# Two PSUM banks per VectorE instruction in the last stage of a recurrence-and-mixture kernel

## The chip, the cores and the metric

The kernel runs on one core of one Trainium2 chip. The metric is the device time of one execution in microseconds, as the median of several runs; lower is better. Beside it there is one profiled execution, whose trace gives the time of every instruction and every DMA packet.

The engines are named as in the profile: PE is TensorE's matrix multiplication (PEld its weight load), DVE is VectorE, ACT is ScalarE, POOL is GpSimd and SP is SyncE, which here only issues DMAs. "SPq L834" is the queue of SP at line 834.

## The reference

Two layers in sequence. The first is a gated recurrence over time; the second is a mixture of experts in which every token is softly assigned to 32 slots (8 experts of 4 slots).

```python
# x, f_logit: (4, 5056, 256); lower_bound: (256,)
sig = 1.0 / (1.0 + np.exp(-f_logit))
f = lower_bound + (1.0 - lower_bound) * sig
for t in range(S):
    h = f[:, t] * h + (1.0 - f[:, t]) * x[:, t]
    y[:, t] = h
# y as (20224, 256); phi: (256, 32); w1: (8, 256, 1024); w2: (8, 1024, 256)
logits = y @ phi
d = softmax of logits over the tokens        # each slot's mix of tokens
slot_out = for each expert e: relu((d.T @ y)[e] @ w1[e]) @ w2[e]
c = softmax of logits over the 32 slots      # each token's mix of slots
out = c @ slot_out                           # (20224, 256), float32
```

The change concerns the last line alone: the 20,224 output rows of 256 floats, 20.71 MB, are products of the tokens' weights (32 numbers a token) with the 32 slot outputs, divided by the sum of the token's weights.

## The kernel before

**Up to the last stage.** `x` and `f_logit` are read in pieces, the recurrence runs as scans on VectorE, and TensorE turns tokens and channels and collects the slots' inputs. The experts follow, in the pools `pm`, `pbig` and others. What the last stage needs then lies in SBUF: `etall`, the exponentials of all logits (128 partitions: 4 batches of 32 slots; one column a position in the sequence); `rrow`, the reciprocals of the row sums; `slot_out`, the slot outputs, repeated for each batch; and `slot_bd`, the same in a two-block layout in which a pair of batches shares 64 partitions, so that one matmul gives the rows of two batches (L759, made by GpSimd).

**How the output is tiled.** `blocks` cuts the sequence of 5056 positions into two blocks of 2048 (`n_r` = 16 rows on each of 128 partitions), one of 896 (`n_r` = 7) and 64 left-over positions. A partition holds `n_r` neighbouring positions, so a store writes `n_r` KB in one piece for each partition.

**What one step does.** TensorE multiplies into one bank of PSUM (128 x 512 floats, 2 KB a partition). Then VectorE or ScalarE reads the bank, multiplies by the reciprocals of the row sums and writes to an SBUF tile. `by_vector` (L765, 766) does a whole bank with one instruction, with the scale as a second operand that is repeated along the row. `by_scalar` (L768 to 770) does one instruction for each row of 256, with the scale as a number for each partition. `next_engine` alternates between the two, bank by bank. When the tile is full, SP issues its store.

**The order**, written out at L853 to 862, is also the order on every engine (the schedule is manual):

1. `pieces(0, 3)`: the first block of batch 3, whose first three rows are stored earlier, in five small stores (10 banks).
2. `couple(2, 0)` and `couple(2, 1)`: the block of 7 rows for batches 0 and 1, then 2 and 3 (7 banks each, two stores of 0.9 MB each).
3. `rest()`: the 64 left-over positions of all batches (2 banks). ScalarE copies half of each bank (L847), VectorE adds the other half (L848), and one VectorE instruction scales them (L849). Two small stores.
4. `whole(0, 2)`: the first block of batch 2 (16 rows, 8 banks of two rows, one store of 2.10 MB).
5. `couple(0, 0)`, `couple(1, 0)`, `couple(1, 1)`: the remaining long blocks in pairs of batches (16 banks of one row of two batches each; two stores of 2.10 MB each).

**Buffers.** `pout` holds 8 tiles of one bank, all of PSUM, handed out in turn by `bank()`. With `reuse_waits="tile"`, a tile of a new pool waits for the earlier users of its own banks and not for everything in the pools that lay there. SBUF holds three tiles for single batches (`ob`) and three for pairs (`oc`), from the pool `osb`.

Of the kernel before, what the change touches and what calls it, by code (L numbers as in the profile page):

```python
# [9 lines left out]
F32 = mybir.dt.float32  # L10
# [4 lines left out]
PSUM = bass.MemoryType.PSUM  # L15
# [3 lines left out]
def kernel(  # L19
# [10 lines left out]
    nc = tc.nc  # L30
    B, S, D = x.shape
    E = moe_w1.shape[0]
    F = moe_w1.shape[2]
    NS = moe_phi.shape[1]
    SPE = NS // E
    P = 128
# [25 lines left out]
    blocks = [(i * P * wide_r, wide_r) for i in range(n_blk)]  # L62
# [57 lines left out]
    etall = store.tile([P, S + PAD], BF16, name="etall")[:, :S]  # L120
    rrow = store.tile([P, n_grp * R, B], F32, name="rrow")
# [6 lines left out]
    slot_bd = store.tile([P, 2, D], BF16, name="slot_bd")  # L128
# [39 lines left out]
    with tc.tile_pool(name="sp2", bufs=3) as sp2, \  # L168
# [430 lines left out]
        for o in range(DC):  # L599
            nc.tensor.matmul(sin_ps[:, o], slot_v[:, o], rep[:, 0],  # L600
                             start=True, stop=True, skip_group_check=True)
# [3 lines left out]
    with tc.tile_pool(name="ew", bufs=1) as ew, \  # L605
# [18 lines left out]
        for q in range(E // Q):  # L624
            hi = ew.tile([P, F], BF16, name=f"hi{q}")
            for k in range(2):
                hi_ps = (psu.tile([P, H], F32, name="hi_ps", tag="up") if q == 0 else
                         pbig.tile([P, H], F32, name="hi_ps", tag=f"hi_ps{k}"))
                for o in range(DC):
                    for j in range(Q):  # L630
                        nc.tensor.matmul(hi_ps[ds(j * NS, NS)], sin[:, o],
                                         w1_sb[q * Q + j][:, o, ds(k * H, H)],
                                         start=(o == 0), stop=(o == DC - 1),
                                         skip_group_check=True)
# [7 lines left out]
        for q in range(E // Q):  # L642
# [6 lines left out]
            k = Q if q == 0 else Q - 1  # L649
# [38 lines left out]
        for i in range(n_late):  # L688
# [3 lines left out]
                             start=True, stop=True, skip_group_check=True)  # L692
# [20 lines left out]
        q = n_grp * R - 1  # L713
        for i in range(len(blocks)):
            expert(Q + i)
            row_sums(i)
            if i < len(blocks) - 1:
                spin(so_ps, 3, D)
                k = ds(i * wide_r, wide_r)
# [3 lines left out]
        k = len(blocks) - 1  # L723
# [39 lines left out]
    with tc.tile_pool(name="osb", bufs=3, reuse_waits="tile") as osb:  # L763

        def by_vector(ob, op, scale):  # L765
            nc.vector.tensor_tensor(ob, op, scale.broadcast_to(list(ob.shape)), ALU.mult)  # L766

        def by_scalar(ob, op, scale):  # L768
            for i in range(ob.shape[1]):
                nc.scalar.activation(ob[:, i], op[:, i], ACT.Copy, scale=scale[:, i])  # L770

        def share(op, i, b, r, k):
            t0, n_r = blocks[i]
            ew = etall[ds(b * NS, NS), ds(t0, P * n_r)].rearrange("s (p r) -> s p r", r=n_r)
            for j in range(k):
                nc.tensor.matmul(op[:, j], ew[:, :, r + j], slot_out[ds(b * NS, NS)],
                                 start=True, stop=True, skip_group_check=True)

        def scale_of(i, b, r, k):
            return rrow[:, ds(blocks[i][0] // P + r, k), ds(b, 1)]  # L780

        def rows_of(i, b):
            t0, n_r = blocks[i]
            return out[ds(b * S + t0, P * n_r)].rearrange("(p r) d -> p r d", r=n_r)

        pout = ctx.enter_context(
            tc.tile_pool(name="pout", bufs=8, space=PSUM, reuse_waits="tile"))

        def bank():
            return pout.tile([P, 2, D], F32, name="op", tag="op")  # L790

        def pieces(i, b):
            dst = rows_of(i, b)
            ob = osb.tile([P, blocks[i][1], D], F32, name="ob", tag="ob")
            for r, ks in ((3, (1, 1)), (5, (1, 1)), (7, (1, 1)), (9, (2, 2)), (13, (2, 1))):
                q = r
                for k, by in zip(ks, (by_vector, by_scalar)):
                    op = bank()
                    share(op, i, b, q, k)
                    by(ob[:, ds(q, k)], op[:, ds(0, k)], scale_of(i, b, q, k))  # L800
                    q += k
                nc.sync.dma_start(out=dst[:, ds(r, q - r)], in_=ob[:, ds(r, q - r)])

        turn = [0]

        def next_engine():
            turn[0] += 1
            return turn[0] % 2

        def whole(i, b):  # L810
            n_r = blocks[i][1]
            ob = osb.tile([P, n_r, D], F32, name="ob", tag="ob")
            for r in range(0, n_r, 2):
                k = min(2, n_r - r)
                op = bank()
                share(op, i, b, r, k)
                (by_scalar, by_vector)[next_engine()](
                    ob[:, ds(r, k)], op[:, ds(0, k)], scale_of(i, b, r, k))
            nc.sync.dma_start(out=rows_of(i, b), in_=ob)

        def couple(i, j):
            t0, n_r = blocks[i]
            ew = etall[ds(j * 2 * NS, 2 * NS), ds(t0, P * n_r)].rearrange(
                "s (p r) -> s p r", r=n_r)
            ob = osb.tile([P, 2, n_r, D], F32, name="oc", tag="oc")
            for r in range(n_r):
                op = bank()
                nc.tensor.matmul(op.rearrange("p u d -> p (u d)"), ew[:, :, r],  # L828
                                 slot_bd[ds(j * 2 * NS, 2 * NS)].rearrange("s u d -> s (u d)"),
                                 start=True, stop=True, skip_group_check=True)  # L830
                (by_scalar, by_vector)[next_engine()](
                    ob[:, :, r], op, rrow[:, t0 // P + r, ds(2 * j, 2)].unsqueeze(2))
            for u in range(2):
                nc.sync.dma_start(out=rows_of(i, 2 * j + u), in_=ob[:, u])  # L834

        def rest():
            n_p = B // 2
            ob = osb.tile([P, n_p, D], F32, name="ob", tag="ob")
            dst = out.rearrange("(b t) d -> t b d", b=B)
            for j in range(n_p):  # L840
                k = ds(j * 2 * NS, 2 * NS)
                op = bank()
                nc.tensor.matmul(op.rearrange("p u d -> p (u d)"),
                                 left[k].rearrange("s t u -> s (t u)"),
                                 slot_bd[k].rearrange("s u d -> s (u d)"),
                                 start=True, stop=True, skip_group_check=True)
                nc.scalar.copy(ob[:, j], op[:, 0])  # L847
                nc.vector.tensor_tensor(ob[:, j], ob[:, j], op[:, 1], ALU.add)  # L848
            by_vector(ob, ob, rrow[:, n_grp * R - 1, ds(0, n_p)].unsqueeze(2))  # L849
            for j in range(n_p):  # L850
                nc.sync.dma_start(out=dst[ds(S - L, L), ds(2 * j, 2)], in_=ob[:, j])

        pieces(0, B - 1)  # L853
        end = len(blocks) - 1
        couple(end, 0)
        couple(end, 1)
        rest()
        whole(0, B - 2)
        for i in range(end):
            for j in range(B // 2):  # L860
                if i or j < B // 2 - 1:
                    couple(i, j)


# [28 lines left out]
```

## Time and profile before

| | |
|---|---|
| median of 3 runs | 197.41 us (197.39 to 197.84) |
| the profiled execution, time | 197.27 us |
| its span, first to last instruction | 195.5 us |
| bytes written | 20.71 MB |
| first packet of the output | 144.04 us from the span's start |
| last packet of the output | 193.1 us |
| last compute instruction | 173.6 us |

Times inside the span count from its start. The page of the profile cuts the span into 40 equal slices of 4.89 us: a row of digits gives for each slice the busy tenths of an engine, the clock that TensorE was granted, or the share of the 16 DMA engines; the row GB/s gives what they moved. A group of instructions reads: line, engine, operation, output<-input by the program's names, shapes, count | busy time, mean ns of one | idle time before them and what ended it. A line of the timeline reads: start, time, engine, line, operation, names, shapes, count, and in brackets the idle time before and what ended it. A line of waits reads: who waited for whom, microseconds in total, times, longest. In the table of windows the columns are the stretch, its length, the busy time (and instructions) of PE, PEld, DVE, ACT and POOL, then the granted clock as a share of full speed, the share of the DMA engines and GB/s.

### The profile page before, as it was taken

The page shows a single profiled execution, that of the slowest core. Times are in us where ns is not written, and L with a number is a line of the kernel's source. Part 1 is how long each engine was busy: PE and PEld are TensorE (multiplying, and loading weights), DVE is VectorE, ACT ScalarE, POOL GpSimd, SP SyncE. Part 2 cuts the span into 40 slices and gives each one's busy share as a digit, 9 for nine tenths or more (in the row PEclk, how much of TensorE's full clock was granted, in tenths as well). Part 3 has the DMA queues.
Part 4 walks back from the last instruction along what each step waited for, and adds up shares of the span by engine and source line. Part 5 has one row for each costly group of instructions (what it writes and reads, how often), then busy time and mean ns, then how long its engine had stood idle before and what let it go on. Part 6 is the DMA issues. An engine that isn't in the chain of part 4 may idle for free.

```text
span 195.5 us, 3277 instructions
## 1 busy us (share of the span) xinstructions
PE 148.4 (76%) x1202; PEld 104.3 (53%) x1202; DVE 144.4 (74%) x187; ACT 141.9 (73%) x200; POOL 101.8 (52%) x79
## 2 busy tenths in 40 slices
PE   0687599977998979899797987998888999920000
PEld 0476468675776767667585866556664334300000
DVE  2669759989699999999999999544287998920000
ACT  3588686899889999999987799434089999950000
POOL 2689578774998688874969979253030000000000
PEclk9999759996999999999999999999999555555555
DMA  6999999999999999999999999999949999999994
GB/s 212 421 417 417 438 427 419 421 427 370 371 427 426 408 333 419 424 416 335 378 420 422 252 215 214 213 215 214 164 182 417 424 431 429 426 429 429 433 433 211
DMA packets 14305, 70.75 MB, mean 362 GB/s; under 512 B 1601, under 2 KB 2882, under 8 KB 10322
## 3 DMA queue, kind: packets, MB, share of 16 engines
q1 hardware_dynamic: 11520, 62.13, 76.8%
q0 software_dynamic: 2768, 8.42, 21.7%
q8 instruction: 9, 0.15, 0.3%
q14 instruction: 6, 0.05, 0.1%
q10 hardware_dynamic: 2, 0.00, 0.0%
HBM read 58.23 MB, written 20.71 MB: 404 GB/s over the span
## 4 chain that ended last, share of the span: by engine, by line
PE 30%; DMA 20%; DVE 16%; POOL 9%; ACT 7%; issue 5%; SPq 1%; POOLq 1%; ACTq 0%; DVEq 0%
DVE h L319 12%; DMA w_t<-in_moe_w_dram 9%; PE op L828 8%; DMA x_t<-in_x_dram 7%; POOL u_t L252 7%; ACT oc L770 5%; PE hp L332 5%; PE sp L267 4%; PE up L273 4%; DMA f_t<-in_f_logit_dram 4%; DVE ht L351 3%; PE slot_ps L189 2%; PE lg L365 2%; POOL w_sb L147 2%; PE slot_ps L416 1%
## 5 line engine op out<-in xcount | busy, mean ns | idle before, releaser
L252 POOL TENSOR_TENSOR u_t<-s_t,x_t 128x1024 bf16<-128x1024 bf16 (+1 forms) x39 | 82.5, 2131 | 22.8 <-ACT s_t L241 11.9
L319 DVE TENSOR_TENSOR_SCAN h<-a,h,up 128x512 bf16<-128x512 f32 (+1 forms) x72 | 86.8, 1252 | 4.5 <-PE up L273 2.2
L241 ACT ACTIVATE s_t<-f_t 128x2048 bf16<-128x2048 f32 (+2 forms) x23 | 38.3, 1668 | 4.7 <-DMA f_t<-in_f_logit_dram 4.6
L332 PE MATMUL hp<-ident_f,h 128*128 128x128 f32 (+1 forms) x160 | 29.5, 309 | 8.0 <-DVE ht L351 6.7
L332 PEld LDWEIGHTS hp<-ident_f,h 128*128 128x128 f32 (+1 forms) x160 | 23.5, 207 | 19.1 <-DVE ht L351 12.7
L267 PE MATMUL sp<-ident_f,s_t 128*128 128x128 f32 x144 | 22.1, 299 | 6.7 <-ACT s_t L241 4.4
L301 ACT ACTIVATE a<-sp,lbs 128x1024 f32<-128x1024 bf16 x24 | 25.4, 1114 | 1.1 <-PE sp L267 1.0
L770 ACT ACTIVATE oc<-op,rrow 128x256 f32<-128x256 f32 x62 | 24.2, 525 | 0.1
L828 PE MATMUL op<-slot_bd,etall 64*128 64x512 bf16 x62 | 22.5, 570 | 0.7 <-POOL slot_bd L759 0.4
L267 PEld LDWEIGHTS sp<-ident_f,s_t 128*128 128x128 f32 x144 | 18.2, 155 | 8.5 <-ACT s_t L241 4.9
L308 ACT ACTIVATE a<-sp,lbs 128x512 f32<-128x512 bf16 (+2 forms) x22 | 17.8, 857 | 4.7 <-PE sp L267 4.4
L766 DVE TENSOR_TENSOR oc<-op,rrow 128x512 f32<-128x512 f32 x31 | 19.8, 683 | 1.6 <-PE op L828 1.6
L273 PE MATMUL up<-ident_f,u_t 64*128 64x64 f32 x192 | 17.7, 231 | 1.8 <-POOL u_t L252 1.8
L189 PE MATMUL slot_ps<-rep,ident_f 128*128 128x256 f32 x52 | 17.5, 432 | 0.0
L273 PEld LDWEIGHTS up<-ident_f,u_t 64*128 64x128 f32 x192 | 14.1, 139 | 5.6 <-POOL u_t L252 2.1
L828 PEld LDWEIGHTS <-etall 64*128 64x128 bf16 x62 | 9.1, 153 | 13.4 <-issue 8.2
L351 ACT COPY ht<-hp 128x512 f32<-128x512 f32 (+1 forms) x20 | 11.7, 583 | 5.5 <-PE hp L332 5.3
L351 DVE COPY ht<-hp 128x512 f32<-128x512 f32 (+1 forms) x20 | 13.4, 669 | 1.4 <-PE hp L332 1.4
L319 DVE TENSOR_TENSOR_SCAN h<-a,up 128x512 bf16<-128x512 f32 x8 | 9.3, 1208 | 2.6 <-ACT a L308 1.7
L365 PE MATMUL lg<-h,phi 128*32 128x512 bf16 (+1 forms) x80 | 9.8, 412 | 0.3 <-ACT et L389 0.2
L267 PE MATMUL up<-ident_f,u_t 128*128 128x128 f32 x48 | 9.4, 327 | 0.7 <-POOL u_t L252 0.7
L189 PEld LDWEIGHTS slot_ps<-rep,ident_f 128*128 128x128 f32 x52 | 8.5, 199 | 1.8 <-issue 0.8
(132 smaller groups left out, 144.9 us busy)
## 6 DMA issues: line engine op xcount, KB each, us to landing
f_t<-in_f_logit_dram SPq DMA_DIRECT2D x12, 1024.0 KB, 12.0
x_t<-in_x_dram SPq DMA_DIRECT2D x12, 1024.0 KB, 11.5
out_dram<-oc SPq DMA_DIRECT2D x6, 2048.0 KB, 13.7
w_sb<-in_moe_w_dram POOLq DMA_DIRECT2D x14, 512.0 KB, 10.2
f_t<-in_f_logit_dram SPq DMA_DIRECT2D x12, 512.0 KB, 8.4
x_t<-in_x_dram SPq DMA_DIRECT2D x12, 512.0 KB, 9.9
out_dram<-oc SPq DMA_DIRECT2D x4, 896.0 KB, 5.7
out_dram<-ob SPq DMA_DIRECT2D x1, 2048.0 KB, 9.2
```

The source lines that it names most:

```text
L189: nc.tensor.matmul(slot_bank[:, 1], ident_f, wide_rep, start=False, stop=False, skip_group_check=True)
L241: nc.scalar.activation(s_t, f_t, ACT.Sigmoid, scale=-1.0)
L252: nc.gpsimd.tensor_tensor(uts[n][:, :r], s_t[:, :r], x_t[:, :r], ALU.mult)
L267: nc.tensor.transpose(ps[:, :, r], t[:, r], ident_f)
L273: nc.tensor.transpose(v[:, :, r], t(r)[k].bitcast(F32), ident_f[k, k])
L301: nc.scalar.activation(a, sp[:, :, :, :, o], ACT.Identity, scale=nomlb[:, ds(o, 1)], bias=1.0)
L319: nc.vector.tensor_tensor_scan(h[:, :T, o], decays[n // 2, o][:, n % 2, :T], up[:, :T, o], hs[number(g - 1, b)][:, ds(used(g - 1) - 1, 1), ...
L332: nc.tensor.transpose(hp[:n_p, r], hw[:, :n_p, r], ident_f)
L351: copy(hts[g][:n_p, b].rearrange("p r d -> p (r d)").bitcast(F32), hps.pop(n)[:n_p].rearrange("p r c -> p (r c)"))
L766: nc.vector.tensor_tensor(ob, op, scale.broadcast_to(list(ob.shape)), ALU.mult)
L770: nc.scalar.activation(ob[:, i], op[:, i], ACT.Copy, scale=scale[:, i])
L828: nc.tensor.matmul(op.rearrange("p u d -> p (u d)"), ew[:, :, r], slot_bd[ds(j * 2 * NS, 2 * NS)].rearrange("s u d -> s (u d)"), start=Tru ...
```

## The change

`pieces`, the couples of the short block and `rest` stay as they are. After `rest` the pool `pout` is closed, and two new pools take its place in PSUM: `singles`, two tiles of one bank, and `doubles`, three tiles of two banks. From there on (`whole` and the three long couples) the banks are not dealt out in turn to the two engines. They follow the list `STEPS` = 1, 2, 2, 1, 2, 1, 2, 2, 1, 2: at a 1, one bank goes to ScalarE (two instructions of 256 elements); at a 2, two banks go to VectorE, which takes them with one instruction of 1024 elements. `whole` runs the first five steps (8 banks of two rows), a long couple all ten (16 banks). VectorE so does 12 rows of 16 and ScalarE 4, where each did 8. The matmuls, the stores and their order are the same; `couple` remains for the short block and `wide_couple` is used for the long ones.

```diff
-        pout = ctx.enter_context(
+        first_banks = ExitStack()
+        pout = first_banks.enter_context(
             tc.tile_pool(name="pout", bufs=8, space=PSUM, reuse_waits="tile"))
...
-        def whole(i, b):
-            n_r = blocks[i][1]
-            ob = osb.tile([P, n_r, D], F32, name="ob", tag="ob")
-            for r in range(0, n_r, 2):
-                k = min(2, n_r - r)
-                op = bank()
-                share(op, i, b, r, k)
-                (by_scalar, by_vector)[next_engine()](
-                    ob[:, ds(r, k)], op[:, ds(0, k)], scale_of(i, b, r, k))
-            nc.sync.dma_start(out=rows_of(i, b), in_=ob)
...
         couple(end, 0)
         couple(end, 1)
         rest()
+        first_banks.close()
+        singles = ctx.enter_context(
+            tc.tile_pool(name="singles", bufs=2, space=PSUM, reuse_waits="tile"))
+        doubles = ctx.enter_context(
+            tc.tile_pool(name="doubles", bufs=3, space=PSUM, reuse_waits="tile"))
+        STEPS = (1, 2, 2, 1, 2) * 2
+
+        def two_banks(k):
+            if k == 1:
+                return singles.tile([P, 1, 2, D], F32, name="one", tag="one")
+            return doubles.tile([P, 2, 2, D], F32, name="two", tag="two")
+
+        def whole(i, b):
+            n_r = blocks[i][1]
+            ob = osb.tile([P, n_r, D], F32, name="ob", tag="ob")
+            r = 0
+            for k in STEPS[:len(STEPS) // 2]:
+                op = two_banks(k).rearrange("p q u d -> p (q u) d")
+                share(op, i, b, r, 2 * k)
+                (by_scalar if k == 1 else by_vector)(
+                    ob[:, ds(r, 2 * k)], op, scale_of(i, b, r, 2 * k))
+                r += 2 * k
+            nc.sync.dma_start(out=rows_of(i, b), in_=ob)
+
+        def wide_couple(i, j):
+            t0, n_r = blocks[i]
+            ew = etall[ds(j * 2 * NS, 2 * NS), ds(t0, P * n_r)].rearrange(
+                "s (p r) -> s p r", r=n_r)
+            ob = osb.tile([P, 2, n_r, D], F32, name="oc", tag="oc")
+            r = 0
+            for k in STEPS:
+                op = two_banks(k)
+                for q in range(k):
+                    nc.tensor.matmul(op[:, q].rearrange("p u d -> p (u d)"), ew[:, :, r + q],
+                                     slot_bd[ds(j * 2 * NS, 2 * NS)].rearrange("s u d -> s (u d)"),
+                                     start=True, stop=True, skip_group_check=True)
+                scale = rrow[:, ds(t0 // P + r, k), ds(2 * j, 2)]
+                if k == 1:
+                    by_scalar(ob[:, :, r], op[:, 0], scale[:, 0].unsqueeze(2))
+                else:
+                    by_vector(ob[:, :, ds(r, k)].rearrange("p u r d -> p r u d"), op,
+                              scale.unsqueeze(3))
+                r += k
+            for u in range(2):
+                nc.sync.dma_start(out=rows_of(i, 2 * j + u), in_=ob[:, u])
+
         whole(0, B - 2)
         for i in range(end):
             for j in range(B // 2):
                 if i or j < B // 2 - 1:
-                    couple(i, j)
+                    wide_couple(i, j)
```

## The prediction

> **What bounds the kernel now.** I read the page first: the slices of the span, to find the stretch that the change touches. Each slice is 4.89 us; `pieces`, the short couples, `rest`, `whole` and the long couples fill the slices from the thirtieth (143 us) on.
>
> ```profile
> span 195.5 us, 3277 instructions
> ...
> PEclk9999759996999999999999999999999555555555
> DMA  6999999999999999999999999999949999999994
> GB/s 212 421 417 417 438 427 419 421 427 370 371 427 426 408 333 419 424 416 335 378 420 422 252 215 214 213 215 214 164 182 417 424 431 429 426 429 429 433 433 211
> ```
>
> From the thirty-first slice on the DMA engines are full: 417, then 424 to 433 GB/s, until the last slice, which is cut short by the end. So the output stage is set by 20.71 MB going out at about 429 GB/s, not by an engine. The waits of SP's queue say the same: at the end it sits 19.1 us on stores alone.
>
> ```profile
> SPq L888 <- DMA out_dram<-oc: 19.1, 1, 19.1
> SPq L834 <- DVE oc L766: 14.6, 5, 4.9
> ```
>
> Compute ends at 173.6 (ScalarE's last), data at 193.1, and the span 2.4 us later. The chain of waits runs through TensorE and ScalarE up to 173 us; that is a chain of releases, and the line above, not the chain, tells that data is what ends late.
>
> A change in compute can therefore cost time only where a store is issued so late that the queue runs dry. I read the timeline of SP, TensorE and VectorE around the change for that margin.
>
> ```profile
> 152.10 1.01 PE L776 MATMUL op<-slot_out,etall 32*128 32x256 bf16 x4 [0.30 <-DVE ob L848]
> 152.41 0.69 DVE L766 TENSOR_TENSOR ob<-ob,rrow 128x512 f32<-128x512 f32 x1
> 153.02 2.48 DVE L766 TENSOR_TENSOR ob<-op,rrow 128x512 f32<-128x512 f32 x4
> ...
> 155.56 1.14 SPq L819 DMA_DIRECT2D out_dram<-ob x1
> 160.62 0.34 SPq L834 DMA_DIRECT2D out_dram<-oc x1
> ```
>
> The last two lines are the issue of `whole`'s store and of the first store of the first long couple. When does the queue need them? Working back from 193.1: three long couples are 3 x 4.19 = 12.58 MB, 29.3 us at 429 GB/s, so their data starts at **163.8**; `whole` is 2.10 MB, 4.9 us, and starts at 158.9. From issue to first packet: the first store of the stage is issued at 143.19 and its first packets are at 144.04, **0.85 us** (the second store takes as long; the first load of the kernel 1.02). So `whole` is issued 2.5 us before it would be missed (158.9 - 0.85 - 155.56), and the long couple **2.3 us** (163.8 - 0.85 - 160.62). The later ones have more: the couples at 167.4 and 173.3 are needed at 173.6 and 183.4, since a couple computes in 6.85 us and moves in 9.77.
>
> **The change, part by part.** The groups by shape give the prices.
>
> ```profile
> L770 ACT ACTIVATE oc<-op,rrow 128x256 f32<-128x256 f32 x62 | 24.2, 525 | 0.1
> L828 PE MATMUL op<-slot_bd,etall 64*128 64x512 bf16 x62 | 22.5, 570 | 0.7 <-POOL slot_bd L759 0.4
> L766 DVE TENSOR_TENSOR oc<-op,rrow 128x512 f32<-128x512 f32 x31 | 19.8, 683 | 1.6 <-PE op L828 1.6
> ...
> L766 DVE TENSOR_TENSOR ob<-op,rrow 128x512 f32<-128x512 f32 x6 | 3.8, 680 | 0.0
> ...
> L766 DVE TENSOR_TENSOR ob<-op,rrow 128x256 f32<-128x256 f32 x3 | 1.1, 416 | 0.0
> ```
>
> *Unchanged.* Bytes, stores, their order and size, and SP's queue: no DMA is added or moved. The matmuls keep number and order. Everything up to `rest` stays. So a gain is excluded: from 144.04 to 193.1 the engines move 20.71 MB, 48.3 us of work at 429 GB/s in 49.05 us, and the 0.75 us lost lies in the small packets before `whole`, which the change leaves alone.
>
> *ScalarE* gets 4 + 3 x 8 = 28 instructions in place of 8 + 3 x 16 = 56. Back to back they start 0.357 us apart, so a long couple costs it 2.9 us instead of 5.7. This is worth nothing: VectorE and TensorE take longer, and the queue longer still.
>
> *VectorE* gets 3 + 3 x 6 = 21 instructions of 1024 elements in place of 4 + 3 x 8 = 28 of 512. The trace has no such instruction. Back to back, 512 elements start 0.598 us apart (four in 2.48 us, the last one 0.68 long). 256 more elements cost 680 - 416 = 264 ns, so 512 more cost 0.53: 1024 elements start **1.13 us** apart and last 1.21. From below: rate alone, 4 x 264 ns, 1.06 us. From above: two of the present ones, 1.20 us, if each bank is paid for. I take 1.13, since the slope is measured on the same operation. `whole` and the first long couple are then 9 x 1.13 = 10.2 us of VectorE, where they were 12 x 0.598 = 7.2 us: **+3.0 us** ahead of a store with a margin of 2.3 us. This is the step that decides.
>
> [...]
>
> *The new pools: a wait is added.* `pieces`, the two short couples and `rest` take 10 + 7 + 7 + 2 = 26 banks of 8 in turn, so `rest` holds the first and second bank. The timeline bears this out: `whole` filled six banks, and its seventh waited until 152.10 for `rest`'s addition on VectorE (L848). The pool `singles` is opened first once `pout` is closed, so its two banks lie there, and the first step of `whole` is a single. `whole`'s first matmul then waits until 152.10, where it ran from 149.92. Queued behind it are all 16 matmuls of `whole` and every later one; ScalarE and VectorE wait for those. Before, the six banks filled early let VectorE start the moment it had finished `rest`, at 153.02. Now: the single (2 matmuls) and the first double (4) start 0.213 us apart at the half clock that holds from 151.6 on, so the last starts at 153.17 and, at 0.416 us each, ends at 153.58. VectorE starts at **153.62, 0.6 us later**. From below 153.02 (0), if the banks lie otherwise; from above +0.33, if every new tile waits for the last reader of the old pool, at 152.38. I take 153.62.
>
> *Does TensorE keep VectorE fed?* `whole`'s second and third doubles are ready at 154.5 and 155.7, before VectorE wants them (154.75, 155.88). In the long couple a matmul starts every 0.427 us and lasts 0.63; the first double is ready at 157.0, the last at 162.55, against 157.0 and 162.7. Eight banks take TensorE 3.41 us and VectorE 3 x 1.13 = 3.39: near enough equal that TensorE costs at most some hundredths. Three double banks cover this; with two, each refill (0.43 + 0.63 us) would stand in the path.
>
> **The sum.** VectorE ends the first long couple at 153.62 + 8 x 1.13 + 1.21 = 163.87 (before: 160.38). SP issues 0.24 us later, as before (160.38 to 160.62), and data flows 0.85 us after that: 164.96. It was needed at 163.8: the queue is empty for **1.15 us**, and since all later data is back to back the end moves by as much. `whole`'s store: VectorE ends at 153.62 + 2 x 1.13 + 1.21 = 157.09, issue at about 157.3, data at 158.15, before 158.9; no loss. Second long couple: 163.87 + 6.8 = 170.7, data could flow at 171.8 and is wanted at 164.96 + 9.77 = 174.7; no loss. The profiled execution took 197.27 us (span 195.5, 1.8 around it), 0.14 under the median of 197.41: 198.42 there, **198.56** as a median.
>
> **The rivals.**
> (a) *The gap closes: not slower.* If VectorE starts at 153.02 the gap is 0.55 us; if the pair of banks also costs 1.06 instead of 1.13, it is gone. It decides from 1.15 us saved over nine instructions and one start. For it: the first price is a bound only; TensorE at full clock (0.108 us apart at 150.9) would fill the first double by 152.9. Against: the windows show the clock at 0.50 from 151.6 on, and 1.06 needs an instruction with no fixed part. Time 197.4 to 197.95. [...]
>
> ```profile
> 150.00:151.00 1.00, 1.00 (x10) 0.95 (x10) 0.24 (x1) 1.00 (x4) 0.00 (x0) 1.00 0.92 387
> 151.00:152.00 1.00, 0.66 (x5) 0.36 (x4) 0.38 (x2) 1.00 (x4) 0.00 (x0) 0.79 1.07 444
> 152.00:153.00 1.00, 0.90 (x4) 0.47 (x3) 0.97 (x3) 1.00 (x4) 0.00 (x0) 0.50 1.06 444
> ```
>
> (b) *One instruction, but paid per bank* (the change does not do what it says): 1.20 instead of 1.13, 9 x 0.07 = 0.6 more: 199.2. With the later start and 1.02 us to the first packet: 199.7.
> (c) *VectorE becomes the bound of the whole stage.* It would have to take 9.77 us for a couple, 1.63 per instruction; then every couple loses time. At 1.8 us: 6 us more up to the first couple's store, then 6 x 0.17 us more for each of two: some 206. Nothing in the rows comes near 1.63.
> (d) *Faster.* Only if bytes moved quicker; the rate of 429 GB/s holds with and without computation beside it (slices 32 to 39).
>
> **How the numbers follow.** A measurement tells 0.3%, 0.6 us, from no change. Forecast (gap of 0.6 to 1.7 us): 0.60. (a): 0.23. (b) and its mixtures: 0.12. (c): 0.03. (d): 0.02. Slower: 0.60 + 0.12 + 0.03 = 0.75; same 0.23, faster 0.02. The range takes in (a) whole and (b) with all its bounds: 197.4 to 199.7.
>
> **What would show it.** Right: 21 VectorE instructions of 1024 elements at about 1.21 us; TensorE idle before `whole`, released by L848 at 152.1; the first long couple issued near 164.1 instead of 160.6; a hole of about 1.1 us in the DMA share near 164 and none later; the end moved by that hole. Wrong: no hole, or the store issued before 162.9; or a hole at each couple (c); or the hole at 158.9, ahead of `whole`, in which case the wait for banks is longer than I have it.

## The result and the profile after

The changed kernel takes 198.31 us (median of 6 runs, 198.05 to 198.64), the kernel before 197.40 us in the runs beside it: a ratio of 1.0044, 95% interval 1.0029 to 1.0059. It is slower by 0.9 us. The forecast was 198.56, slower.

The profiled execution of the changed kernel took 198.46 us. First the slices of its span, 4.92 us each:

```profile
span 196.7 us, 3241 instructions
...
DMA  5999999999999999999999999999869997999996
GB/s 201 398 420 421 433 427 422 427 427 375 365 425 427 408 332 427 422 413 332 381 420 419 243 213 213 214 213 215 142 223 418 423 434 320 427 427 427 427 427 267
```

The stage that had 417 to 433 GB/s throughout now has one slice of 320, the thirty-fourth (162.3 to 167.2 us). The windows around it, columns as before (PE, PEld, DVE, ACT, POOL, granted clock, DMA share, GB/s):

```profile
163.00:164.00 1.00, 1.00 (x4) 0.38 (x3) 1.00 (x2) 0.56 (x2) 0.00 (x0) 0.50 1.19 508
164.00:165.00 1.00, 1.00 (x4) 0.44 (x3) 1.00 (x2) 0.60 (x2) 0.00 (x0) 0.50 0.01 0
165.00:166.00 1.00, 1.00 (x4) 0.33 (x2) 1.00 (x2) 0.10 (x1) 0.00 (x0) 0.50 0.61 262
166.00:167.00 1.00, 1.00 (x4) 0.39 (x3) 1.00 (x2) 0.74 (x2) 0.00 (x0) 0.50 1.26 524
```

The row of 164 us is the hole: no data starts, while TensorE and VectorE are busy all the time. By the packets, no DMA engine moves anything from 164.46 to 165.59, **1.13 us**; there is no other hole of this size. From the start of its first packet to the end of its last the stage takes 50.59 us for 49.64 before, 0.95 more. Besides, the stage started 0.34 us later in this execution (first packet at 144.38 for 144.04), before the changed code.

The timeline of TensorE, VectorE and SP around it:

```profile
152.76 0.58 PE L776 MATMUL one<-slot_out,etall 32*128 32x256 bf16 x2 [2.84 <-DVE ob L838]
```

```profile
152.74 0.69 DVE L766 TENSOR_TENSOR ob<-ob,rrow 128x512 f32<-128x512 f32 x1
154.22 3.49 DVE L766 TENSOR_TENSOR ob<-two,rrow 128x1024 f32<-128x1024 f32 x3 [0.80 <-PE two L776]
157.79 12.59 DVE L766 TENSOR_TENSOR oc<-two,rrow 128x1024 f32<-128x1024 f32 x11
```

```profile
157.77 0.35 SPq L870 DMA_DIRECT2D out_dram<-ob  x1
164.75 15.24 SPq L892 DMA_DIRECT2D out_dram<-oc  x6
```

TensorE stands still for 2.84 us until `rest`'s addition (L838, which was L848) gives the bank free; VectorE then waits 0.80 us for TensorE; the first long couple's store is issued at 164.75, and its first packet is the end of the hole, 0.84 us later. The groups by shape answer to those of before:

```profile
L766 DVE TENSOR_TENSOR oc<-two,rrow 128x1024 f32<-128x1024 f32 x18 | 20.5, 1215 | 0.1
L881 PE MATMUL two<-slot_bd,etall 64*128 64x512 bf16 x36 | 17.1, 627 | 0.1
L770 ACT ACTIVATE oc<-one,rrow 128x256 f32<-128x256 f32 x24 | 10.1, 470 | 9.8 <-PE one L881 9.1 <-issue 0.6
```

An instruction over two banks takes 1.215 us (1.21 was worked out); VectorE has no idle time in the long couples, and ScalarE is idle for half of them without harm.

### The profile page after: what moved, and what is told of

Same layout as the page of the kernel before. It is cut to its first block, busy times and chain, and to the rows that moved or that the text cites. A ratio compares the mean times of both kernels' runs of the same rounds, so it can differ in the third digit from the quotient of the medians.

```text
span 196.7 us, 3241 instructions
## 1 busy us (share of the span) xinstructions
PE 149.8 (76%) x1202; PEld 105.0 (53%) x1202; DVE 150.6 (77%) x180; ACT 132.2 (67%) x172; POOL 101.4 (52%) x79
## 4 chain that ended last, share of the span: by engine, by line
DMA 24%; DVE 23%; PE 22%; POOL 9%; issue 7%; ACT 3%; SPq 2%; DVEq 1%; POOLq 1%; ACTq 0%
DVE h L319 12%; DMA x_t<-in_x_dram 12%; DMA w_t<-in_moe_w_dram 9%; POOL u_t L252 6%; DVE oc L766 6%; PE hp L332 4%; PE up L273 4%; DMA out_dram<-ob 3%; PE sp L267 3%; DVE ht L351 3%; ACT oc L770 2%; PE slot_ps L189 2%; PE lg L365 2%; POOL w_sb L147 2%; SPq L231 2%
## 5 line engine op out<-in xcount | busy, mean ns | idle before, releaser
L766 DVE TENSOR_TENSOR oc<-two,rrow 128x1024 f32<-128x1024 f32 x18 | 20.5, 1215 | 0.1
L881 PE MATMUL two<-slot_bd,etall 64*128 64x512 bf16 x36 | 17.1, 627 | 0.1
L770 ACT ACTIVATE oc<-one,rrow 128x256 f32<-128x256 f32 x24 | 10.1, 470 | 9.8 <-PE one L881 9.1
L881 PEld LDWEIGHTS <-etall 64*128 64x128 bf16 x48 | 7.4, 161 | 12.0 <-issue 9.9
```

What stands on the lines that cost most here:

```text
L881: nc.tensor.matmul(op[:, q].rearrange("p u d -> p (u d)"), ew[:, :, r + q], slot_bd[ds(j * 2 * NS, 2 * NS)].rearrange("s u d -> s (u d)"), ...
```

## The experiments

All of them ask what makes that one store late, and whether anything but the store matters. Since the stage starts at a slightly different time in each execution, the issue of the first long couple's first store is given **from the first output packet**: 16.58 us before, 20.38 in the changed kernel. The hole is the time without packets ahead of that store's data; the stage is the time from the first output packet to the end of the last. All three are from one profiled execution, the median is over the timed runs. The ratio is the one on record, to the kernel before in the same session (medians 197.51 for pool alone, pools the other way round, late couples only and half stores, 197.53 for the other four); it is not exactly the quotient of the two medians.

| kernel | store issued | hole | stage | median us | ratio, 95% interval |
|---|---|---|---|---|---|
| before | 16.58 | 0 | 49.64 | 197.40 | |
| changed | 20.38 | 1.13 | 50.59 | 198.31 | 1.0044 (1.0029 to 1.0059) |
| pool alone | 19.45 | 0.22 | 49.69 | 197.57 | 1.0008 (0.9992 to 1.0024) |
| pools the other way round | 19.95 | 0.75 | 50.16 | 197.96 | 1.0023 (1.0010 to 1.0036) |
| free banks first | 19.77 | 0.25 | 49.98 | 197.42 | 0.9990 (0.9978 to 1.0002) |
| late couples only | 17.05 | 0 | 49.58 | 197.60 | 1.0011 (0.9993 to 1.0029) |
| half stores | 16.97 | 0 | 49.82 | 197.40 | 0.9987 (0.9972 to 1.0002) |
| half share | 21.27 | 1.54 | 51.48 | 198.63 | 1.0055 (1.0034 to 1.0075) |
| bank by bank | 21.44 | 1.72 | 51.66 | 199.12 | 1.0065 (1.0044 to 1.0087) |
| all on VectorE | 23.13 | 3.99 | 53.34 | 201.21 | 1.0176 (1.0153 to 1.0198) |

**Is it the store, or the engines?** (Half stores.) The first long couple stores in halves; no engine's work changes.

```diff
-        def wide_couple(i, j):
+        def wide_couple(i, j, halves=False):
...
                 r += k
+                if halves and r in (n_r // 2, n_r):
+                    q = ds(r - n_r // 2, n_r // 2)
+                    for u in range(2):
+                        nc.sync.dma_start(out=rows_of(i, 2 * j + u)[:, q], in_=ob[:, u, q])
...
-                    wide_couple(i, j)
+                    wide_couple(i, j, i == 0)
```

> The changed kernel, but the first long couple stores each batch in two halves of 8 rows (four stores of 1.05 MB for two of 2.10 MB, 8 KB packets for 16 KB), the first two as soon as 8 rows are done. No engine's work changes. Theory (all of the loss is the queue running dry before that couple's store): the first half is issued near 161, before the queue is empty, no hole: 197.4, or up to 0.2 more for the smaller packets. Rival (the loss is in the engines, or contention of VectorE with the DMA): 198.3 as in the changed kernel.

The first half goes out 16.97 us after the first packet instead of 20.38, the hole is gone, and so is the loss: 197.40. The timeline of SP in this run:

```profile
157.80 0.35 SPq L870 DMA_DIRECT2D out_dram<-ob  x1
161.37 5.05 SPq L894 DMA_DIRECT2D out_dram<-oc  x4
```

VectorE's instructions stand where they stood in the changed kernel (whole at 9.85 us after the first packet in both), so neither the two-bank reads nor a contention of theirs with the DMA, if there is one, cost anything that the timed runs resolve (a ratio of 0.9987 to the kernel before, 0.9972 to 1.0002). The 0.9 us is the queue running dry. By the same ratio the smaller packets cost nothing that these runs resolve.

**Is it one store, or the pace of the stage?** (Late couples only.) `whole` (its function as in the kernel before) and the first long couple run as before, the last two couples as in the change.

```diff
         rest()
+        def whole(i, b):
...
+        whole(0, B - 2)
+        couple(0, 0)
         first_banks.close()
...
-        whole(0, B - 2)
-        for i in range(end):
+        for i in range(1, end):
             for j in range(B // 2):
-                if i or j < B // 2 - 1:
-                    wide_couple(i, j)
+                wide_couple(i, j)
```

> whole and the first long couple as in the kernel before, the new pools and the three-quarter share only in the last two long couples. Theory (only the store of the first long couple is late; later ones have 6 us and more in hand): no hole, 197.4 within 0.2. Rival (VectorE, or a cost of two-bank reading, sets the pace of the stage): two of the three couples still cost, 198.0 or more.

No hole, and 197.60 can't be told from before. Two thirds of the long couples with three quarters of their data on VectorE cost nothing that the runs resolve (a ratio of 1.0011, 0.9993 to 1.0029): VectorE doesn't set the pace of the stage.

**A larger dose.** (All on VectorE.) Four double banks, everything on VectorE.

```diff
-        singles = ctx.enter_context(
-            tc.tile_pool(name="singles", bufs=2, space=PSUM, reuse_waits="tile"))
         doubles = ctx.enter_context(
-            tc.tile_pool(name="doubles", bufs=3, space=PSUM, reuse_waits="tile"))
-        STEPS = (1, 2, 2, 1, 2) * 2
+            tc.tile_pool(name="doubles", bufs=4, space=PSUM, reuse_waits="tile"))
+        STEPS = (2, 2, 2, 2) * 2
...
```

> The changed kernel with four double banks and all of whole and the long couples on VectorE: 12 instructions up to the first long couple's store in place of nine. Theory: VectorE sets the end of that couple, 12 x 1.13 us from about 9.2 us after the first packet: store issued near 22.9 to 23.2, hole of 3.7 to 4.0 us, and none later, since a couple then costs VectorE 9.05 us and the DMA 9.77: 200.9 to 201.4. Rival (some of the lateness is taken up by the queue, or later couples lose as well): less than 200, or a second hole and over 202.

Issued at 23.13, hole 3.99, 201.21 us: every part as expected. Three of its windows, the second of which stands for the four without data (164 to 168 us):

```profile
163.00:164.00 1.00, 0.98 (x2) 0.28 (x2) 1.00 (x2) 0.00 (x0) 0.00 (x0) 0.50 0.99 426
...
166.00:167.00 1.00, 0.88 (x3) 0.30 (x2) 1.00 (x2) 0.00 (x0) 0.00 (x0) 0.50 0.00 0
...
178.00:179.00 1.00, 0.88 (x3) 0.30 (x2) 1.00 (x2) 0.00 (x0) 0.00 (x0) 0.50 1.23 524
```

Store lateness turns into time one to one, from a fixed point on. From the issue of that store to the end of the stage it takes 30.21 to 30.24 us in all seven kernels with a hole (stage less issue in the table). The stage before takes 49.64 us, so a store issued later than 49.64 - 30.21 = **19.43 us** costs what it is later, and the margin was 19.43 - 16.58 = **2.85 us**. The hole alone overstates the loss: it is 0.2 to 0.3 us longer than what the stage loses here, in the changed kernel and in the next two (1.13 for 0.95 in the changed kernel); why is left open.

**The wait for banks alone.** (Pool alone.) The split of before, but from `whole` on with banks of a new pool.

```diff
...
         rest()
+        first_banks.close()
+        pools.append(ctx.enter_context(
+            tc.tile_pool(name="plate", bufs=8, space=PSUM, reuse_waits="tile")))
         whole(0, B - 2)
```

> The split of the kernel before (bank by bank in turn, half the data on each engine), but whole and the long couples take their banks from a new pool of eight, opened after rest. TensorE then waits for rest's banks as in the changed kernel. Theory (the store of the first long couple has a margin of 2.3 us, whatever eats it): TensorE starts the first long couple about 2.9 us later than before (155.9 for 153.0), at its own pace of 0.427 us a matmul the store is issued near 163.6 for 160.6, a hole of 0.4 to 0.8 us in the DMA: 197.8 to 198.2. Rival (VectorE's larger load is the whole cost and the wait for banks is covered): no hole, 197.4.

TensorE is held up exactly as in the changed kernel: the first long couple's matmuls start at 11.87 us after the first packet (9.00 before, 11.88 changed) and the last at 18.29 (15.41; 18.29).

```profile
152.59 1.65 PE L776 MATMUL op<-slot_out,etall 32*128 32x256 bf16 x7 [2.41 <-DVE ob L849]
```

The store goes out at 19.45, 2.87 us later than before, and the hole is 0.22 us, half of the lower end expected. The time misses the expectation as well: 197.57 lies below 197.8 to 198.2 and can't be told from before, which is the rival's number. Its reason is not borne out, though. The wait isn't covered, it uses up the whole margin; the margin is 2.85 and not 2.3, and so almost nothing is lost beyond it.

**The share alone, first try.** (Pools the other way round.) Pools the other way round, and the doubles meant to start at the second.

```diff
-        singles = ctx.enter_context(
-            tc.tile_pool(name="singles", bufs=2, space=PSUM, reuse_waits="tile"))
         doubles = ctx.enter_context(
             tc.tile_pool(name="doubles", bufs=3, space=PSUM, reuse_waits="tile"))
+        singles = ctx.enter_context(
+            tc.tile_pool(name="singles", bufs=2, space=PSUM, reuse_waits="tile"))
+        doubles.tile([P, 2, 2, D], F32, name="two", tag="two")
```

> The changed kernel with its two pools laid the other way round and the double banks started at the second of the three, so that rest's two banks are wanted last (for the third double of whole). TensorE no longer waits for rest before it starts whole. Theory: VectorE starts on whole as soon as it has finished rest, some 0.9 us earlier than in the changed kernel, and its nine instructions then end about 163.3 on the clock of the profile before; the hole shrinks from 1.13 to 0.2 to 0.5 us: 197.6 to 197.9. Rival (VectorE's load is the whole cost): the hole stays at 1 us or more, 198.3. Rival (the wait for banks is the whole cost): no hole, 197.4.

The edit did half of what it was meant to. The tile that is never used didn't move the turn, so the first double lay on one of `rest`'s banks. The timeline of TensorE shows the single going early and the double waiting:

```profile
150.06 0.64 PE L776 MATMUL one<-slot_out,etall 32*128 32x256 bf16 x2
152.66 1.86 PE L776 MATMUL two<-slot_out,etall 32*128 32x256 bf16 x8 [1.96 <-DVE ob L838]
```

VectorE starts `whole` 9.43 us after the first packet (9.85 changed, 8.98 before): half of the delay is left, and a hole of 0.75 with it. The time of 197.96 lies just above the 197.6 to 197.9 expected.

The placement in the compiled programs explains this. `rest`'s two tiles lie in bank 7 (its first) and bank 0 (its second). In the changed kernel the singles are banks 0 and 1 and the doubles 2-3, 6-7 and 4-5, in this order; so the first single waits for the second addition of `rest`, the later of the two. Here the first double is 0-1.

**The share alone, second try.** (Free banks first.) The two singles are dealt out in the other order, bank 1 first; then neither the first single nor the first double lies on a bank of `rest`.

```diff
-        singles = ctx.enter_context(
-            tc.tile_pool(name="singles", bufs=2, space=PSUM, reuse_waits="tile"))
+        singles = [ctx.enter_context(
+            tc.tile_pool(name=f"single{i}", bufs=1, space=PSUM, reuse_waits="tile"))
+            for i in range(2)]
+        taken = [0]
...
-                return singles.tile([P, 1, 2, D], F32, name="one", tag="one")
+                taken[0] += 1
+                return singles[taken[0] % 2].tile([P, 1, 2, D], F32, name="one", tag="one")
```

> The changed kernel with the two single banks dealt out in the other order, so that the first single and the first double of whole lie on banks that rest doesn't hold (in the run with the pools the other way round the first double still lay on one). VectorE should then start whole as soon as rest is done, 0.87 us sooner than in the changed kernel. Theory (hole = time by which the couple's store is issued after 19.2 us from the first packet; so far 19.45 gave 0.22, 19.95 gave 0.75, 20.38 gave 1.13): issue near 19.3 to 19.6, hole 0.1 to 0.4 us, 197.5 to 197.8. Rival (VectorE's load alone makes the loss): hole of 0.7 or more, 198.1 or more.

197.42 us, not to be told from before and under the 197.5 to 197.8 expected, with three quarters of the data on VectorE and two banks for each instruction. TensorE waits for the last short couple alone, and VectorE goes from `rest` into `whole` without a gap (153.04 + 0.61):

```profile
152.01 0.58 PE L776 MATMUL one<-slot_out,etall 32*128 32x256 bf16 x2 [1.49 <-ACT oc L770]
```

```profile
153.04 0.69 DVE L766 TENSOR_TENSOR ob<-ob,rrow 128x512 f32<-128x512 f32 x1
153.65 3.48 DVE L766 TENSOR_TENSOR ob<-two,rrow 128x1024 f32<-128x1024 f32 x3
```

The profiled execution was among the longer ones (197.73); its stage lost 0.34 us, with a hole of 0.25 at this store. In it TensorE's granted clock fell to half 1.7 us after the first packet, as the short couples began (7.9 us in the changed kernel), and VectorE starts `whole` at 9.41 us for 8.98 before. An execution without these 0.43 us would issue the store at about 19.34, an estimate from 19.77, which is just ahead of 19.43. So the work alone uses up nearly all of the margin, too.

**Half the share, two banks at a time.** (Half share.)

```diff
-        STEPS = (1, 2, 2, 1, 2) * 2
+        STEPS = (1, 1, 2, 1, 1, 2) * 2
```

> The changed kernel with the steps 1, 1, 2: VectorE takes half the data, still two banks with an instruction, ScalarE the other half bank by bank. TensorE starts late as in the changed kernel. Theory (late start and the long last instruction, which can't begin before both banks are written and takes 1.21 instead of 0.69 us, are enough; VectorE's share hardly adds): TensorE ends the first long couple 18.9 us after the first packet, store issued near 20.2, hole of 0.9 to 1.1 us, 198.2 to 198.4. Rival (three quarters on VectorE are the cost): hole of 0.2 us as with the pool alone, 197.6.

198.63: giving VectorE a third less work doesn't bring the time back. This profiled execution too had the early halving (TensorE starts `whole` at 9.05 instead of 8.38 us after the first packet; it took 199.46, far above the median), so its store and its hole are some 0.7 us later and larger than without it. In it VectorE is idle before 12 of the long couples' instructions:

```profile
L766 DVE TENSOR_TENSOR oc<-two,rrow 128x1024 f32<-128x1024 f32 x12 | 14.7, 1225 | 6.5 <-PE two L881 6.5
```

TensorE's last matmul of the first couple starts 19.32 us after the first packet and lasts 0.63; VectorE's last instruction runs from 19.98 to 21.21, and the store follows. So TensorE sets the end, and the last instruction comes on top with its full 1.2 us.

The median lies 0.2 us above the expected 198.4, and the trace shows a delay that the edit brought with it. Half of the data now goes through the two single banks, and three times TensorE waits for ScalarE to free one. Of the pairs of single banks, the one at 158.82 waits and the next doesn't:

```profile
158.82 1.21 PE L881 MATMUL one<-slot_bd,etall 64*128 64x512 bf16 x2
160.68 1.05 PE L881 MATMUL one<-slot_bd,etall 64*128 64x512 bf16 x2
```

In the first of the two, ScalarE's last instruction on the bank wanted ends at 159.39, and TensorE's second matmul starts at 159.44. From the first matmul of `whole` to the last of the couple TensorE takes 10.27 us for 9.91 in the changed kernel. Without these 0.36 us and the early halving the store would be issued at about 21.27 - 0.67 - 0.36 = 20.24, an estimate, which still costs 0.8 us. The pool-alone kernel has the same wait and the same share and issues at 19.45: by this estimate the 0.8 us between are the price of ending on a two-bank instruction.

**Three quarters, bank by bank.** (Bank by bank.) VectorE takes each bank of a double by itself, in `whole` too.

```diff
...
-                    by_vector(ob[:, :, ds(r, k)].rearrange("p u r d -> p r u d"), op,
-                              scale.unsqueeze(3))
+                    for q in range(k):
+                        by_vector(ob[:, :, r + q], op[:, q], scale[:, q].unsqueeze(2))
```

> The changed kernel, but VectorE takes the two banks of a double with two instructions of 512 elements. Its eighteen instructions for whole and the first long couple at 0.598 us are 0.6 us more work than nine at 1.13, but each can start when its own bank is written, 0.4 us sooner at the start. Theory: store issued near 20.3 us after the first packet, hole about 1.1 us, 198.3 as in the changed kernel. Rival (reading two banks with one instruction is dear in itself): hole clearly smaller, 197.8 or less.

199.12, 0.8 us above the changed kernel: a miss of the expectation of 198.3. The rival, which wanted 197.8 or less, is out as well. The head start that I counted on doesn't exist. VectorE's first instruction begins at 10.53 us after the first packet, when both banks of the double are written, as with one instruction; then its 18 instructions run without a gap (10.53 + 17 x 0.598 + 0.68 = 21.4; issue at 21.44). The store is issued 1.06 us later than in the changed kernel. Of this, 0.68 is VectorE's later start, since this execution had the early halving as well; 0.38 is the eighteen instructions, which take 10.85 us where the nine take 10.47. How much of the 0.8 us in the median belongs to each is open. Reading two banks with one instruction isn't dear in itself: it saves these 0.38 us.

## Why the prediction was right, point by point

- **The bound and the place of the loss: right.** One hole, ahead of the first long couple's store, none at `whole` and none later; the end moves by it, less 0.18 us.
- **The margin: mis-sized.** I worked back from 193.1 us as the end of the data, and the table of times has it as the last packet. But 193.1 is where the last packet starts; it ends at 193.68. From there the same steps give 2.9 us for 2.3, and the stores themselves put the margin at 2.85. The loss came out 0.5 us too large by this.
- **The price of two banks: right.** 1.215 us for one, 1.13 to 1.14 apart.
- **The wait for banks: right in kind, under-sized.** TensorE was released by `rest`'s addition, but by the second one, since the first single lies on the bank of `rest`'s second tile. VectorE's start moved by 0.87 us (8.98 to 9.85), not 0.6: close to the upper bound that I gave (0.93).
- **"The step that decides": too narrow.** I put the loss on VectorE's 3.0 us more work. But neither delay costs anything alone that the runs resolve: not that work without the wait (free banks first), and not the wait with the old split (pool alone). Together they cost 0.9 us. With the wait, a third less work doesn't bring the time back either (half share). I had asked only whether TensorE keeps VectorE fed, and not where the store would be with less work. In the changed kernel TensorE is done at 18.29 + 0.63 = 18.92, so a last instruction of 1.21 can end at 20.13 at best; VectorE ends at 20.32. VectorE's chain does end last, as the sum has it, but TensorE's is only 0.2 us behind, and as long as the couple ends on a two-bank instruction, less work on VectorE can win back no more than that.
- **The sum: right in its terms, near by luck.** The 1.15 us were 0.6 (start) + 2.89 (VectorE's time from its start to the end of the couple, 10.25 for 7.36) - 2.34 (margin). Measured: 0.87 + 3.11 - 0.18 - 2.85 = 0.95. The 3.11 hold 0.2 more than was worked out, most of it where TensorE passes from `whole` to the couple (VectorE's fourth instruction starts 1.30 us after the third). The 0.18 is SP: I took the 0.24 us between VectorE's end and the issue before as SP's own, but there ScalarE ended last, 0.03 us ahead of the issue; in the changed kernel VectorE ends last and SP follows after 0.06. Four errors of 0.2 to 0.5 us came to -0.2 in all. The terms earned the direction and the rough size; that the forecast lies only 0.25 us off is luck.
- **The rivals.** (a) didn't happen, but its first price (VectorE starting with no delay) is the free-banks kernel: I left a loss of 0.55 us there, and with the margin as measured almost none is left, as the runs show. TensorE at full clock, which I had counted for (a), was not to be had in the changed kernel either: TensorE had been idle for 2.4 us (149.9 to 152.3) when the granted clock fell to 0.50. (b) is out by the 1.13 us, (c) by the late-couples kernel, (d) by the longer time.

## What to carry to other kernels

In a stage that a full DMA queue bounds, as here (417 to 433 GB/s in the nine slices from the thirty-first before the change), an engine's time counted only up to the next store: work out for each store how long before it is missed it is issued, and compare the sum of all added delays with that margin. Here either of two delays, of about 2.8 and 2.9 us, cost nothing that the runs resolve, and both together cost 0.9 us. Take the end of the last packet, not its start, when you work back. Opening a new pool on old buffers put a wait at the place where the first tiles land (2.84 us of TensorE); look where the last users of those banks are, and hand out the free banks first. Where the store got late, a smaller first store (issued at 16.97 us for 20.38) mended it at no cost that these runs resolve (197.40 us).

## What the runs showed of the hardware that was not expected

The moment at which TensorE's clock falls to half wanders against the kernel: 7.6 and 7.9 us after the first output packet in the profiled executions before and after and 8.2 with half stores, 1.4 to 1.7 in three experiments, 2.8 to 3.9 in four others. In the three with the earliest fall the stores of the short couples are 0.4 to 0.9 us later than before, and small holes of 0.16 to 0.43 us open there. The windows of the free-banks kernel show the half clock from 146 us, with TensorE busy 0.57 of the microsecond before and all of the one after:

```profile
145.00:146.00 1.00, 0.57 (x5) 0.37 (x4) 1.00 (x3) 1.00 (x4) 0.63 (x1) 0.98 1.01 377
146.00:147.00 1.00, 1.00 (x5) 0.36 (x5) 0.93 (x3) 0.88 (x4) 0.00 (x0) 0.50 1.05 404
```

That this makes part of the spread between runs (197.2 to 198.0 us for most) is likely, since the three profiled executions with the earliest fall were among the longer of their kernels, but it was not tried by itself.
